# New cost figures for the list scheduler of a mixer block: attention and gated MLP in one kernel

## The chip, the cores and the metric

The kernel runs on one core of a Trainium2 chip. The core has five engines with instruction queues of their own: TensorE (PE, matrix products), VectorE (DVE), ScalarE (ACT), GpSimd (POOL) and SyncE (SP, here only an issuer of DMAs). They meet through semaphores. The metric is the time of one execution on the device in microseconds (us), smaller being better; of several executions the median is given.

## The reference

Two branches share one layer-normalized input and are added to it:

```python
xn = _layernorm(x)                       # x: (1, 2048, 512) bf16
# A: 32 heads of 16; each position attends to 8 earlier ones, 2 apart
q, k, v = split(xn @ wqkv)               # wqkv: 512 x 1536
logits[h, s, w] = sum_d q[h, s, d] * k[h, s - 2*w, d] * 0.25   # w = 0..7, masked before 0
o[h, s] = sum_w softmax(logits)[h, s, w] * v[h, s - 2*w]
A = o @ wo                               # 512 x 512
# B: gelu, a gate that mixes positions, projection
z = gelu(xn @ w_in)                      # 512 x 1792, halves z1 and z2 of 896
g = w_sp @ _layernorm(z2) + b_sp         # w_sp: 2048 x 2048, over positions
B = (z1 * g) @ w_out                     # 896 x 512
out = x + A + B
```

## The kernel before

The 2048 positions are 16 blocks b of 128, or 4 groups j (also called tc) of 512. The program is written as a list of tasks, each with an engine, the keys that it reads and writes, an estimate of its time (`est`) and a name. `Plan.add` turns the keys into dependences. `Plan.schedule` (from line 95) then fixes the order of the tasks on every engine; nothing is reordered at run time. Each engine runs its tasks strictly in that order and waits on semaphores where a dependence is not met, so a task that waits holds up everything behind it on its engine. A DMA is a task of the engine that issues it.

The scheduler keeps a clock for each engine. Again and again it takes, over all engines, the task that can start first by these clocks; of those that could start within `slack` of one another it prefers the class with the lower number (`prio`; the class FILL comes after the default), and then the order in which the tasks were written. A task may carry a `margin`, which is added to the time at which its inputs are ready. `plan.orders` fixes a few orders at the very start by hand. The estimates therefore don't change what an instruction costs on the chip, only who stands before whom.

The work and its names, in the order in which it comes (lines are those of the kernel before):

- **Front.** `ldx` (L533) loads a block of x; `bnst`, `bnag` (L598, L601, DVE), `rstd` (L603, a power on POOL) and `norm` (L605, DVE) normalize it. For blocks 0 to 3 PE transposes (`xTr`, L620), for 4 to 15 the DMA does: `xTd`, L609, issued by SP.
- **Products of xn.** On PE, in this order: `z2_b` (L785) with gelu on ACT (`z2g`, L790, with an accumulated sum; `z2s`, L812, a sum of squares); `Q`, `K` (L665), evicted by ACT (`QKe`, L673); `V` (L647), evicted by ACT (`Ve`, L651) and written to a scratch in memory by POOL's queue (`Vw`, L654); later `z1` (L802) with gelu (L807). `halo` (L679) copies 16 columns on POOL. The layer norm of z2 is `zm`, `zq`, `ze`, `zv` (L818 to L828, DVE), `zr` (L831, a power on POOL) and `zn` (L834, DVE).
- **Attention scores on DVE**, for each group j: four `prod` (L689) and three `padd` (L694), all 128x4096; then a transpose of 1 MB by DMA, `pT` (L706, SP); then `dd0`, `dd1` (L714, L717), the softmax (`sm`, `ssub`, `sexp` on ACT, `sz`, `srec`, `sattn`: L729 to L766) and a trip through memory, `aw` and `al` (L768, L772, POOL's queue).
- **The gate.** `g{fc}_{tc}` (L908) is one group of 16 matmuls over all positions, 7 groups for each tc, 28 in all. Each needs a PSUM bank that ACT has seeded with the bias (`gs`, L902), and w_sp transposed by DMA: `wT` (L841, SP, 2 MB for each tc, in two slots, so that `wT2` waits until group 6 of tc 0 is done, and `wT3` for group 6 of tc 1). `u{fc}_{tc}` (L915, DVE) multiplies the result into z1 and frees the bank; from tc 1 on the groups share four banks.
- **Attention output**, for each j and par in 0, 1: `ldVe` (L925, ACT's queue, 1152 KB) loads V with its shifts; `pv` (two, L933), `pva2048` and `pva1024` (L937) and `pvc` (L941) on DVE form o; `OTd{j}_{par}` (L946, SP, 256 KB) transposes it for two output blocks.
- **Output blocks.** `out{b}` is 4 matmuls with wo (L974) and 7 with w_out (L978), onto a bank that ACT seeds with x (`ldxr`, L962, and `os`, L969); `fin` (L987) evicts and `st` (L990) stores. Blocks 0 and 2 of a group j need `OTd{j}_0`, blocks 1 and 3 `OTd{j}_1`; all need the seven `u` of group j.

SP's queue in the later part reads, in both kernels: ... `pT2`, `ldwout`, four `ldwo`, `wT2`, `pT3`, `OTd0_0`, `wT3`, `OTd0_1`, `OTd1_0`, `OTd1_1`, `OTd2_0`, `OTd2_1`, `OTd3_0`, `OTd3_1`, last store.

Of the kernel before, what the change touches and what calls it, by code (L numbers as in the profile page):

```python
# [6 lines left out]
ENGS = ("pe", "act", "dve", "pool", "sp")  # L7
# [7 lines left out]
class Plan:  # L15
# [79 lines left out]
    def schedule(self, lookahead=64, slack=120.0, dma_bw=300.0, xbar_bw=190.0,  # L95
                 dma_lat=1700.0, issue_ns=None, inv_tol=None, sw_bias=1300.0, verbose=False):
        inv_tol = inv_tol or {"dve": 2400.0}
        issue_ns = issue_ns or {"sp": 650.0, "act": 650.0, "pool": 660.0}
        pending = {e: {} for e in ENGS}
        for t in self.tasks:  # L100
            pending[t.eng].setdefault(t.prio[0], []).append(t)
        for e in ENGS:
            for c in pending[e]:
                pending[e][c].sort(key=lambda t: t.prio)
        byname = {t.name: t for t in self.tasks}
        before = {}
        for names in self.orders:
            for a, b in zip(names, names[1:]):
                assert byname[a].eng == byname[b].eng
                before.setdefault(byname[b], []).append(byname[a])  # L110
        eng_free = {e: 0.0 for e in ENGS}
        dma_free = {e: 0.0 for e in ENGS}
        dma_glob = [0.0]
        order = {e: [] for e in ENGS}
        remaining = len(self.tasks)

        def lat(d, t):
            if d.dma is not None:
                return 150.0
            if d.eng == t.eng:  # L120
                return 35.0
            return 210.0 if d.eng == "pe" else 80.0

        cur_tbl = [None]

        def dur(t):
            if t.dma is not None:
                return issue_ns.get(t.eng, 650.0)
            if t.tbl is not None and t.tbl != cur_tbl[0]:
                return t.est + 1300.0  # L130
            return t.est

        while remaining:
            best = None
            for e in ENGS:
                pl = []
                for c in pending[e]:
                    pl.extend(pending[e][c][:lookahead])
                if not pl:
                    continue  # L140
                cands = []
                for t in pl:
                    ok = all(p.start is not None for p in before.get(t, ()))
                    ready = 0.0
                    for d in t.deps:
                        if d.end is None:
                            ok = False
                            break
                        r = d.end + lat(d, t)
                        if r > ready:  # L150
                            ready = r
                    if ok:
                        st_ = max(eng_free[e], ready + t.margin)
                        if t.tbl is not None and t.tbl != cur_tbl[0] and cur_tbl[0] is not None:
                            st_ += sw_bias
                        cands.append((st_, t))
                if not cands:
                    continue
                pick = None
                pool_c = list(cands)  # L160
                while pool_c:
                    mn = min(c[0] for c in pool_c)
                    near = [c for c in pool_c if c[0] <= mn + slack]
                    P = min(near, key=lambda c: (c[1].prio, c[0]))
                    pend = P[0] + dur(P[1])
                    viol = False
                    for c in cands:
                        if c[1].prio[0] < P[1].prio[0] and pend > c[0] + inv_tol.get(e, 300.0):
                            viol = True
                            break  # L170
                    if not viol:
                        pick = P
                        break
                    pool_c.remove(P)
                if pick is None:
                    pick = min(cands, key=lambda c: (c[1].prio[0], c[0], c[1].prio))
                if best is None or (pick[0], pick[1].prio) < (best[0], best[1].prio):
                    best = pick
            if best is None:
                raise RuntimeError("scheduler stuck (dependency cycle?)")  # L180
            st, t = best
            e = t.eng
            if t.tbl is not None and t.tbl != cur_tbl[0] and cur_tbl[0] is not None:
                st -= sw_bias
            t.start = st
            if t.dma is not None:
                iss = issue_ns.get(e, 650.0)
                t.eng_end = st + iss
                bw = xbar_bw if t.dma.get("xbar") else dma_bw
                xs = max(st + 0.5 * iss, dma_glob[0])  # L190
                xe = xs + t.dma["nbytes"] / bw
                dma_glob[0] = xe
                t.end = max(xe, st + iss) + t.dma.get("lat", dma_lat)
            else:
                t.eng_end = st + dur(t)
                t.end = t.eng_end
                if t.tbl is not None:
                    cur_tbl[0] = t.tbl
            eng_free[e] = t.eng_end
            pending[e][t.prio[0]].remove(t)  # L200
            order[e].append(t)
            remaining -= 1
        self.order = order
        self.makespan = max(t.end for t in self.tasks)
        if verbose:
            self.report()
        return order
# [107 lines left out]
def build_kernel(nc, A_x, A_wqkv, A_wo, B_x, B_w_in, B_w_sp, B_b_sp, B_w_out, out, report=False, sched_kw=None,  # L315
# [12 lines left out]
    FILL = cfg["fill"]  # L328
# [66 lines left out]
    with ExitStack() as es:  # L395
# [92 lines left out]
            return max(25.0, n / 2.4 + 2.6)  # L488

        def c_act(n, psum=True, accum=False):  # L490
            return 165.0 + n * (0.84 if psum else 0.84) + (110.0 if accum else 0.0)

        def c_dve(n, mode=1.0):
            return 130.0 + n / (0.96 * mode)
# [3 lines left out]
        def dma(eng, fn, nbytes, chan, reads=(), writes=(), name="", xbar=False, prio=None, lat=1700.0):  # L498
# [10 lines left out]
          name="steps0")  # L509
# [147 lines left out]
        def qk_pair(j, c):  # L657
            k = next_pair()
            for which in range(2):
                col0 = which * 512 + c  # L660

                def mm(t, col0=col0, which=which):
                    last = None
                    for dc in range(4):
                        last = t.matmul(bank(k + which), AC(off["wqk"] + 1024 * dc + col0, [[4, 128]]),  # L665
                                        AC(off["xnT"] + dc * S + 512 * j, [[1, 512]]), start=(dc == 0),
                                        stop=(dc == 3))
                    return last
                T("pe", mm, reads=[(("wq", "wk")[which], c)] + [("xnT", b) for b in range(4 * j, 4 * j + 4)],
                  writes=[("ps", k + which)], est=4 * c_mm(512), name="%s%d_%d" % ("QK"[which], j, c))  # L670
            qo = q_off(c, j)
            ko = k_off(c, j)
            T("act", lambda a: a.activation(AC(qo, [[ko - qo, 2], [1, 512]]),  # L673
                                            ps[:, 512 * k: 512 * k + 1024].rearrange("p (t n) -> p t n", t=2),
                                            ACTF.Copy, scale=0.5),
              reads=[("ps", k), ("ps", k + 1)], writes=[("QT", c, j), ("KT", c, j)], est=c_act(1024),
              name="QKe%d_%d" % (j, c))
            if j < NJ - 1:
                T("pool", lambda g: g.tensor_copy(AC(k_off(c, j + 1) - KP, [[1, KP]]), AC(ko + 512 - KP, [[1, KP]])),  # L679
                  reads=[("KT", c, j)], writes=[("KTpad", c, j + 1)], est=150, name="halo%d_%d" % (j, c))  # L680

        def prod_reduce(j):
            pa, pb, pc, pl = [(j + i) % NPB for i in range(4)]
# [132 lines left out]
        def z2_wave(j):  # L816
# [12 lines left out]
                                               ALU.subtract),  # L829
              reads=[("msq", j)], writes=[("vpe2", j)], est=160, name="zv%d" % j)  # L830
            T("pool", lambda g: g.tensor_tensor(Fv("rstd2", 4, 4 * j), Fv("vpe2", 4, 4 * j), mhalf, ALU.pow),  # L831
              reads=[("vpe2", j), "mhalf"], writes=[("rstd2", j)], est=900, name="zr%d" % j)
            for b in bl:
                T("dve", (lambda b: lambda v: v.tensor_scalar(A("z2", FH, FH * b), A("z2", FH, FH * b),  # L834
                                                              Fv("m2", 1, b), Fv("rstd2", 1, b), ALU.subtract,
# [84 lines left out]
        def pv_pair(j, par):  # L920
# [3 lines left out]
                          ap=[[4 * 512, 128], [1024, 9], [1, 512]])  # L924
            dma("act", lambda e: e.dma_start(AC(off["Ve"] + 4608 * par, [[512, 9], [1, 512]]), src),  # L925
                128 * 4608 * 2, ("Ve", par), reads=[("vscr", i) for i in range(4 * j - 1, 4 * j + 4)],
                writes=[("Ve", par)], name="ldVe%d_%d" % (j, par), prio=FILL, lat=3400.0)
            nm = "%d_%d" % (j, par)
            for i in range(2):
                iv = AC(off["Ve"] + 4608 * par + (7 + i) * 512, [[-512, 8], [32, 16], [1, 32]])  # L930
# [5 lines left out]
            for n in (2048, 1024):  # L936
# [9 lines left out]
            dma("sp", lambda e: e.dma_start_transpose(AC(off["OT"] + 512 * ob, [[128, 8], [1, 128]]),  # L946
                                                      A("On", 1024, 1024 * so)),
                128 * 1024 * 2, ("OTd", so), reads=[("On", so)], writes=[("OT", ob), ("OT", ob + 1)], name="OTd" + nm,
                xbar=True, lat=3600.0)

        def ot_pos(b):
            return 4 * (b // 4) + 2 * (b % 2) + (b % 4) // 2
# [3 lines left out]
        def out_block(tb, parts=(512,)):  # L956
# [7 lines left out]
            for p_, n in enumerate(parts):  # L964
# [7 lines left out]
                def mm(t, c0=c0, po=po, n=n):  # L972
# [7 lines left out]
                    return last  # L980
                T("pe", mm, reads=[("z1T", fc, tcb) for fc in range(FC)] + ["w_out", ("OT", ot_pos(tb))] + [("wo", c) for c in range(4)],
                  writes=[("ps", k)], est=(FC + 4) * c_mm(n), name="out%d_%d" % (tb, p_),
                  margin=2500.0)
                last_part = p_ > 0
                T("dve" if last_part else "act",
                  (lambda c0, po, n: lambda v: v.tensor_copy(A("yout", n, 512 * sx + c0), po))(c0, po, n) if last_part else
# [82 lines left out]
```

## Time and profile before

| | us |
|---|---|
| median of 3 runs (lowest, highest) | 237.55 (237.34, 238.16) |
| the profiled execution, its own time | 236.66 |
| span of its trace | 234.9 |
| PE busy, share of the span | 231.0, 98% |
| DVE busy | 202.8, 86% |
| ACT busy | 117.5, 50% |
| POOL busy | 50.1, 21% |
| granted TensorE clock | 1.0 |

The page gives busy time by engine, the chain of work that ended last, groups of instructions by line, and the DMA issues with their time to landing. "Idle before, releaser" is what an engine waited for. A time like 145.9 is counted from the start of the span. SPq and ACTq are the queues of SP and ACT as issuers of DMAs: the length of such a row is how long the engine was held by the issue, and the landing comes later.

### The profile page before, as it was taken

To read this page: it belongs to the slowest core of one execution; us is meant where nothing else is said; L and a number is where in the kernel's file an instruction comes from. 1 tells how busy PE (TensorE), PEld (TensorE's weight loads), DVE (VectorE), ACT (ScalarE), POOL (GpSimd) and SP (SyncE) were. 2 spreads that over 40 slices of the span, in tenths; PEclk is the share of its full clock that TensorE was granted. 3 is DMA by queue.
4 is the path that set the end of the run, shared out by engine and by line. 5 is a ranking of instruction groups with operands and counts; after the bars stand their busy time and mean duration, and the time that the engine had idled before them with its cause. 6 is when DMAs were issued, how large, how long until landed. Compare 5 with 4: busy or idle time off the path is not lost.

```text
span 234.9 us, 2932 instructions
## 1 busy us (share of the span) xinstructions
PE 231.0 (98%) x1094; PEld 109.8 (47%) x1094; DVE 202.8 (86%) x230; ACT 117.5 (50%) x227; POOL 50.1 (21%) x67
## 2 busy tenths in 40 slices
PE   7999999999999999999999999999999999999995
PEld 2454455454554444444444444444444444444443
DVE  4789889998989989998999992999999999999600
ACT  2798478998989978962011232324124161201441
POOL 4446944680780050001301000010000000000000
PEclk9999999999999999999999999999999999999999
DMA  7998997390209999796439999999855789702322
GB/s 225 276 360 174 233 225 191 99 171 0 91 3 178 220 231 265 105 253 233 132 87 222 192 312 235 242 181 323 216 156 142 197 268 203 197 3 45 88 69 67
DMA packets 87021, 41.75 MB, mean 178 GB/s; under 512 B 66000, under 2 KB 85856, under 8 KB 87008
## 3 DMA queue, kind: packets, MB, share of 16 engines
q1 hardware_dynamic: 70928, 23.24, 46.5%
q10 hardware_dynamic: 14640, 14.13, 20.8%
q0 software_dynamic: 1440, 4.21, 6.6%
q8 instruction: 8, 0.13, 0.3%
q14 instruction: 5, 0.04, 0.1%
HBM read 20.05 MB, written 5.26 MB: 108 GB/s over the span
## 4 chain that ended last, share of the span: by engine, by line
PE 95%; DMA 2%; DVE 1%; SPq 1%; POOL 0%; issue 0%
PE ps L908 41%; PE ps L665 12%; PE ps L978 10%; PE ps L802 10%; PE ps L785 9%; PE ps L974 6%; PE ps L647 6%; DMA arena<-in_A_x_dram 2%; POOL fpool L603 0%; DVE arena L605 0%; SPq L543 0%; SPq L533 0%; DVE fpool L598 0%; PE ps L620 0%; DVE fpool L601 0%
## 5 line engine op out<-in xcount | busy, mean ns | idle before, releaser
L908 PE MATMUL ps<-arena 128*128 128x512 bf16 x448 | 97.3, 379 | 0.0
L908 PEld LDWEIGHTS ps<-arena 128*128 128x128 bf16 x448 | 43.8, 98 | 52.8
L902 ACT ACTIVATE ps<-arena 128x512 f32<-128x512 bf16 x28 | 16.5, 599 | 57.4 <-DVE arena L915 57.3
L933 DVE TENSOR_TENSOR arena<-arena 128x4096 bf16<-128x4096 bf16 x16 | 36.2, 2286 | 0.4
L689 DVE TENSOR_TENSOR arena<-arena 128x4096 bf16<-128x4096 bf16 x16 | 36.1, 2284 | 0.3 <-ACT arena L673 0.2
L665 PE MATMUL ps<-arena 128*128 128x512 bf16 x128 | 28.3, 379 | 0.0
L937 DVE TENSOR_TENSOR arena<-arena 128x4096 bf16<-128x4096 bf16 (+1 forms) x16 | 28.0, 1753 | 0.2
L694 DVE TENSOR_TENSOR arena<-arena 128x4096 bf16<-128x4096 bf16 x12 | 27.4, 2287 | 0.2
L978 PE MATMUL ps<-arena 128*128 128x512 bf16 (+2 forms) x119 | 27.0, 366 | 0.0
L785 PE MATMUL ps<-arena 128*128 128x448 bf16 x128 | 25.5, 353 | 0.1
L802 PE MATMUL ps<-arena 128*128 128x512 bf16 x112 | 24.3, 379 | 0.0
L665 PEld LDWEIGHTS ps<-arena 128*128 128x128 bf16 x128 | 14.5, 113 | 13.1
L987 ACT ACTIVATE arena<-ps 128x512 bf16<-128x512 f32 (+1 forms) x16 | 9.4, 586 | 21.5 <-PE ps L978 18.6
L673 ACT ACTIVATE arena<-ps 128x1024 bf16<-128x1024 f32 x16 | 16.4, 1022 | 5.7 <-PE ps L665 5.0
L915 DVE TENSOR_TENSOR arena<-ps,arena 128x512 bf16<-128x512 f32 x28 | 19.0, 680 | 0.0
L790 ACT ACTIVATE arena<-ps 128x448 bf16<-128x448 f32 x32 | 17.3, 543 | 2.4
L978 PEld LDWEIGHTS ps<-arena 128*128 128x128 bf16 x119 | 13.1, 113 | 11.4
L785 PEld LDWEIGHTS ps<-arena 128*128 128x128 bf16 x128 | 12.2, 98 | 11.8 <-ACT arena L626 0.6
L807 ACT ACTIVATE arena<-ps 128x512 bf16<-128x512 f32 x28 | 15.9, 595 | 3.2 <-PE ps L802 2.7
L802 PEld LDWEIGHTS ps<-arena 128*128 128x128 bf16 x112 | 11.0, 98 | 13.1
L974 PE MATMUL ps<-arena 128*128 128x512 bf16 (+2 forms) x68 | 16.6, 366 | 0.1
L679 POOL COPY arena<-arena 128x16 bf16<-128x16 bf16 x12 | 14.3, 1197 | 9.9 <-DVE arena L689 7.7
(61 smaller groups left out, 189.2 us busy)
## 6 DMA issues: line engine op xcount, KB each, us to landing
arena<-vscr ACTq DMA_DIRECT2D x8, 1152.0 KB, 7.1
arena<-in_A_x_dram ACTq DMA_DIRECT2D x17, 128.0 KB, 6.1
vscr<-arena POOLq DMA_DIRECT2D x16, 128.0 KB, 2.4
arena<-in_A_x_dram SPq DMA_DIRECT2D x15, 128.0 KB, 4.5
out_dram<-arena ACTq DMA_DIRECT2D x15, 128.0 KB, 3.2
arena<-in_A_wqkv_dram SPq DMA_DIRECT2D x3, 512.0 KB, 5.2
ascr<-arena POOLq DMA_DIRECT2D x4, 256.0 KB, 4.5
arena<-ascr POOLq DMA_DIRECT2D x4, 256.0 KB, 3.7
```

The lines of the kernel that those rows point to most:

```text
L665: last = t.matmul(bank(k + which), AC(off["wqk"] + 1024 * dc + col0, [[4, 128]]), AC(off["xnT"] + dc * S + 512 * j, [[1, 512]]), start=(dc ...
L689: T("dve", lambda v: v.tensor_tensor(pbv, qb, kb, ALU.mult), reads=[("QT", c, j), ("KT", c, j), ("KTpad", c, j)], writes=[("pb", s_)], est ...
L694: T("dve", lambda v: v.tensor_tensor(A("pb", 4096, 4096 * a), A("pb", 4096, 4096 * a), A("pb", 4096, 4096 * b), ALU.add), reads=[("pb", b) ...
L785: last = t.matmul(ps[:, 512 * k: 512 * k + HF], AC(off["xnT"] + dc * S + 128 * b, [[1, 128]]), AC(off["w_in"] + 1792 * dc + c0, [[1, HF]]) ...
L790: T("act", (lambda k, hf: lambda a: a.activation(A("z2", HF, FH * b + HF * hf), ps[:, 512 * k: 512 * k + HF], ACTF.Gelu_apprx_tanh, accum_ ...
L802: lastm = t.matmul(bank(k), AC(off["w_in"] + 1792 * dc + 128 * fc, [[1, 128]]), AC(off["xnT"] + dc * S + 512 * j, [[1, 512]]), start=(dc = ...
L908: last = t.matmul(bank(k), AC(off["z2"] + FH * sh + 128 * fc, [[1, 128]]), AC(off["wT"] + WSL * r_ + sh * 512, [[1, 512]]), start=False, s ...
L915: T("dve", lambda v: v.tensor_tensor(uv, bank(k), uv, ALU.mult), reads=[("ps", k)], writes=[("z1T", fc, tc)], est=c_dve(512) + 20, name="u ...
L933: T("dve", (lambda iv, tv, av: lambda v: v.tensor_tensor(tv, iv, av, ALU.mult))(iv, tv, av), reads=[("attn", j), ("Ve", par)], writes=[("V ...
L937: T("dve", (lambda n: lambda v: v.tensor_tensor(AC(off["Vs"], [[4096, 2], [1, n]]), AC(off["Vs"], [[4096, 2], [1, n]]), AC(off["Vs"] + n, ...
L974: t.matmul(po, AC(off["OT"] + 512 * ot_pos(tb) + 128 * cc, [[1, 128]]), AC(off["wo"] + 512 * cc + c0, [[1, n]]), start=False, stop=False, ...
L978: last = t.matmul(po, AC(off["z1T"] + fc * S + t0, [[ts, 128]]), AC(off["w_out"] + 512 * fc + c0, [[1, n]]), start=False, stop=(fc == FC - ...
```

## The change

Only figures of the scheduler change; no instruction is added, removed or changed in shape. The diff, whole in its code:

```diff
-        issue_ns = issue_ns or {"sp": 650.0, "act": 650.0, "pool": 660.0}
+        issue_ns = issue_ns or {"sp": 470.0, "act": 420.0, "pool": 600.0}
...
-        eng_free = {e: 0.0 for e in ENGS}
+        eng_free = {e: 730.0 for e in ENGS}
...
             if t.dma is not None:
+                if t.dma.get("xbar"):
+                    return max(1250.0, 400.0 + 0.0046 * t.dma["nbytes"])
                 return issue_ns.get(t.eng, 650.0)
...
-                iss = issue_ns.get(e, 650.0)
+                iss = dur(t)
                 t.eng_end = st + iss
-                bw = xbar_bw if t.dma.get("xbar") else dma_bw
-                xs = max(st + 0.5 * iss, dma_glob[0])
-                xe = xs + t.dma["nbytes"] / bw
-                dma_glob[0] = xe
-                t.end = max(xe, st + iss) + t.dma.get("lat", dma_lat)
+                if t.dma.get("xbar"):
+                    dma_glob[0] = max(st, dma_glob[0]) + t.dma["nbytes"] / 450.0
+                    t.end = max(dma_glob[0], st + iss) + 2000.0
+                else:
+                    xs = max(st + 200.0, dma_glob[0])
+                    xe = xs + t.dma["nbytes"] / 340.0
+                    dma_glob[0] = xe
+                    t.end = max(xe, st + iss) + t.dma.get("lat", dma_lat)
...
-            return 165.0 + n * (0.84 if psum else 0.84) + (110.0 if accum else 0.0)
+            return 165.0 + n * (0.84 if psum else 0.84) + (200.0 if accum else 0.0)
...
-                  reads=[("KT", c, j)], writes=[("KTpad", c, j + 1)], est=150, name="halo%d_%d" % (j, c))
+                  reads=[("KT", c, j)], writes=[("KTpad", c, j + 1)], est=1200, name="halo%d_%d" % (j, c))
...
-              reads=[("vpe2", j), "mhalf"], writes=[("rstd2", j)], est=900, name="zr%d" % j)
+              reads=[("vpe2", j), "mhalf"], writes=[("rstd2", j)], est=2500, name="zr%d" % j)
...
-                writes=[("Ve", par)], name="ldVe%d_%d" % (j, par), prio=FILL, lat=3400.0)
+                writes=[("Ve", par)], name="ldVe%d_%d" % (j, par), prio=FILL, lat=2600.0)
...
                 128 * 1024 * 2, ("OTd", so), reads=[("On", so)], writes=[("OT", ob), ("OT", ob + 1)], name="OTd" + nm,
-                xbar=True, lat=3600.0)
+                xbar=True)
...
-                  margin=2500.0)
+                  margin=1500.0)
```

What moves on each engine, by name:

- **PE**: everything up to `g6_1` keeps its place. Before, the order behind it is `g0_2 g1_2 g2_2 out0 out2 g3_2 g4_2 g5_2 g6_2 out1 out3 g0_3 out4 out6 out5 out7 g1_3` and so on. After, it is `out0 out2 g0_2 g1_2 g2_2 g3_2 out1 out3 g4_2 g5_2 g6_2 out4 out6 out5 out7 g0_3 g1_3` and so on. From `g1_3` on the two are the same.
- **DVE**: in the front several `norm`, `bnst` and `bnag` come ahead of `prod0_0`; in the three later waits for `zr1` to `zr3` a `prod`, `padd` or `dd` is put between `zv` and `zn`. In the gate stage the order shifts by one or two places: `padd3_1` stands ahead of `u6_0`; `u1_2` and `u2_2` stand behind `pvc0_1`; `u5_2` and `u6_2` behind `pvc1_1`.
- **ACT**: `QKe` come ahead of `z2s`; `ldVe0_1` moves from the gate stage to just behind `ldVe0_0`; in the gate stage `os0_0` stands ahead of `gs5_1`, `ldVe1_0` behind `os3_0`, and `ldxr4` to `ldxr7` ahead of `gs0_2`.
- **POOL**: some `rstd` and `halo` change places, `al0` comes ahead of `aw1`.
- **SP**: `ldx9` ahead of `ldw_in1`, `xTd5` ahead of `ldx12`, `ldx14` and `ldbbc` behind `xTd11`, `xTd15` ahead of `xTd14`. From `pT0` on the order is the same.

## The prediction

> **What bounds the kernel now.** First the busy times of the page, by engine:
>
> ```profile
> PE 231.0 (98%) x1094; PEld 109.8 (47%) x1094; DVE 202.8 (86%) x230; ACT 117.5 (50%) x227; POOL 50.1 (21%) x67
> ```
>
> PE is busy for all but 3.9 us of a span of 234.9. Next the chain of work that ended last (start, length, what):
>
> ```profile
> 10.34 0.40 PE ps L620 x4
> 10.73 3.03 PE ps L785 x16
> ...
> 97.53 58.71 PE ps L908 x272
> 156.24 0.86 PE ps L974 x4
> 157.10 1.51 PE ps L978 x7
> ...
> 187.75 0.06 issue
> 187.81 1.02 PE ps L974 x4
> 188.84 1.51 PE ps L978 x7
> ```
>
> From 10.34, when the first transpose of normalized x runs, to 232.48 the chain is PE and nothing else, and it is broken once, for 0.06 us ahead of `out5`. One group `g` takes 58.71 / 272 x 16 = 3.45 us, one output block 0.86 + 1.51 = 2.37. The matmuls are the same after the change. So their 222 us stay, what lies in front stays (the orders of SP, DVE, ACT and PE are unchanged up to PE's start), and the last store stays behind `out15`. The change can win only the gap at `out5`; it can lose wherever PE, in its new order, comes to a task whose inputs are not there. The question is which inputs are late.
>
> Third, SP's queue in time order, and VectorE around its one long wait in the gate stage:
>
> ```profile
> 121.73 11.73 SPq L841 DMA_TRANSPOSE arena<-in_B_w_sp_dram  x1
> 133.51 9.78 SPq L706 DMA_TRANSPOSE arena<-arena  x1
> 143.34 2.12 SPq L946 DMA_TRANSPOSE arena<-arena  x1
> 145.91 9.90 SPq L841 DMA_TRANSPOSE arena<-in_B_w_sp_dram  x1
> ```
>
> ```profile
> 139.62 2.28 DVE L933 TENSOR_TENSOR arena<-arena 128x4096 bf16<-128x4096 bf16 x1
> 146.50 1.23 DVE L714 TENSOR_TENSOR arena<-arena 128x2048 bf16<-128x2048 bf16 x1 [4.60 <-DMA arena<-arena]
> ```
>
> The 2 MB `wT2` (L841) may start only when `g6_0` is done, at 97.53 + 7 x 3.45 = 121.7. Issuing it holds SP for 11.73 us, `pT3` (L706) behind it for 9.78, and `OTd0_0` (L946), whose input DVE had ready at 139.06 (`pvc0_0`, 138.37 + 0.69), is issued at 143.34. The trace gives its landing 3.9 us later, 147.28. DVE waits until 146.50 for `pT3` to land. In the old order `out0` reads this transpose at 156.24, 9 us later.
>
> **Part by part.**
>
> *Front and products of xn (up to 97.53).* DVE loses three waits of 0.9 us for `zr1` to `zr3` (2.8 us at L834, released by POOL) and some of the waits for loads, about 1 us by stepping the new order through the old durations; it reaches `padd2_2` some 2 to 4 us earlier. PE gets nothing from that: it never waited for DVE there. Could PE now wait? The last transposes of xn landed at 40.6, and `V12` reads them at 56.95; `xTd14`, now last, is issued about 5 us later than the old last one at most, so 10 us are left. `ldVe0_0` and `ldVe0_1` stand ahead of `QKe1_2` on ACT and wait for `Vw3` (landed at 30.62; `QKe1_2` ran at 32.79): two issues of 0.38 us, below the 3.45 us that two of the eight banks cover. `zn15`, done at 88.4, comes at about 90, due at 97.53. I cost all this at nothing. If one cover failed it would be by parts of a us; with the range below I allow 0 to +0.5.
>
> *Start of tc 1.* `padd3_1` now stands ahead of `u6_0`. `u5_0` waits for `g5_0` (118.25); then 0.6 + 0.65 + 0.95 + 0.6 for the softmax tail and 2.2 for `padd3_1` put `u6_0` at 123.3, done at 124.0, and `gs1_1`, which needs that bank, at 124.6. `g1_1` starts at 97.53 + 8 x 3.45 = 125.16. That leaves 0.5 us: no hold, but the cover is thin; 1 us more on DVE would cost 0.5.
>
> *`out0` and `out2` moved ahead of `g0_2`.* PE reaches `out0` after 14 groups, at 97.53 + 14 x 3.4535 = 145.88. `OTd0_0` stands in the same place of SP's queue, behind the same `wT2`, whose start PE sets at 121.7, and the same `pT3`. VectorE's earlier start doesn't help: SP, not `padd3_2` or `pvc0_0`, is late. Landing again at 147.28, it holds PE. What a hold costs beyond the landing the trace shows at `out5`: the transpose landed at 187.68, the first matmul began at 187.81 (0.13 later), and four matmuls took 1.02 instead of 0.86, since the pipeline was empty. So the hold is 147.28 + 0.13 - 145.88 + 0.16 = **1.69 us**, and nothing behind hides it, because PE runs without gaps to the end.
> The scheduler's new figures say why it dares: a transpose's issue is 400 + 0.0046 x bytes, so 5.2 us for `pT3` and 10.0 for `wT2`; the trace has 9.78 and 11.73 there, 6.3 us more in sum. The figure fits `pT0`, `pT1` (4.88, 4.68), which ran while ACT loaded nothing.
>
> *`out1`, three groups earlier.* Due at 164.44, and at 166.13 with the first hold. `OTd0_1` waits for `pvc0_1`. DVE starts from the same 146.50 and was never idle from there to 182; the new order takes `u1_2` and `u2_2` out of the way: from start to start, one saves 0.48 (2.20 + 0.60 with a `u` between `pva2048` and `pva1024` against 2.32 without), the other 0.42 (0.87 + 0.54 with it behind `srec`, against 0.99). `pvc0_1` ends at 162.27 - 0.90 = 161.37; with the 4.2 us that this transpose took, it lands at 165.6. Not held, by 0.5 us.
>
> *`out5`, one group earlier.* Due at 184.30, with the hold 185.99. `pvc1_1` ends about 0.87 earlier than 182.03 (again two `u` fewer before it), and `OTd1_1`, issued at 181.2, lands 3.0 to 5.6 us later (the fastest and this one in the trace), 184.2 to 186.8. I take no hold: the small loads and stores that ran beside it (`ldxr9`, `ldxr11`, `st1`, `st3`) now come before. Then the old gap, 0.22 with its empty pipeline, is gone. At the other end it is 1.1 us.
>
> *Rest.* The four gate banks of tc 3 are freed over 5 us ahead (`u0_3` ends at about 198, `g4_3` starts at 206); `OTd3_1` landed at 224.44 and `out13` starts at 227.69. Nothing.
>
> *The unknown: how fast `pT3` goes.* It was issued at 133.51 and landed 13.0 us later; `pT0` took 6.8. Beside it ran `ldVe1_0` (1152 KB, issued at 133.83) and the tails of `ldxr0` to `ldxr3`. In the new order these four loads are issued some 2.5 us earlier (`padd3_2` ends at 126.2, not 128.80), `ldVe1_0` behind them and `os3` at 134 to 138, and `ldxr4` to `ldxr7` follow at once, 0.52 MB more. If `pT3` has the engines to itself for a while it may land 2 to 4 us earlier; if the 0.52 MB go first, at the 309 GB/s of the window from 133.5 to 143.3, it lands 1.7 later. I take no change, which is the nearest row (same neighbour, same size), and keep both ends.
> [...]
>
> **Sum.** +1.69 - 0.22 = +1.47. The profiled execution took 236.66, 0.89 below the median of 237.55, so it goes to 238.13, the median to 239.0.
>
> **Rivals.**
> (a) *Not slower.* `pT3` lands at 145.5 or earlier, because `ldVe1_0` starts after it: `OTd0_0` then lands by 146, the hold is 0.4 or none, and only the gap at `out5` goes: -0.2 to +0.7, 237.35 to 238.25. For it: `pT0`'s 6.8 us. Against: `wT2` still moved until 137.4, and `ldVe1_0` needs only `pv0_0_1`, which is earlier too. It decides from 1 us on at `pT3`.
> (b) *Two holds.* `pT3` and `OTd0_0` are slowed by the loads that now follow `ldVe1_0`, by 1.7, or `out5` is held too, by 1.1: 1.47 + 1.1 = +2.6 to 1.47 + 1.7 = +3.2, and with the half us of the front up to +3.7: 240.1 to 241.3. For it: `OTd1_1` is the one transpose that was late before.
> (c) *The change does not do what it says*: figures closer to the trace should give an order with fewer waits, and DVE's waits do shrink; but no wait that shrinks is PE's, and a gain of over 0.7 us (236.8 and below) would need PE to start earlier or to have less work. I see nothing for it but the scatter of the median.
>
> **How the numbers follow.** 0.3% of 237.55 is 0.71 us, about what a measurement of this kernel can tell from no change. Forecast (+0.7 to +2.6): 0.50. Rival (a): 0.20. Rival (b): 0.26. Rival (c): 0.04. Slower is the forecast and (b), 0.76; same is (a), 0.20; faster (c), 0.04. The range takes in (a) and (b) to their ends: 237.3 to 241.3.
>
> **What would show it.** In the profile after: a gap of PE at 145.9 ahead of `out0` (L974 in the old lines), ended by the DMA, and the chain going through SP's queue there. `OTd0_0`'s landing at about 147.3; DVE again idle to 146.5 for `pT3`. No gap at `out1`; at `out5` none or below 1 us. PE's start at 10.3 and everything up to 145.9 without gaps. I am wrong if `pT3`'s issue takes clearly less than 9.8 us, or if PE has gaps before 125, where I found none.

## The result and the profile after

The changed kernel took **240.88 us** (median of 10 runs, 239.19 to 241.56) against 237.57 for the kernel before (10 runs, 236.4 to 238.3): ratio **1.0134** (95% interval 1.0101 to 1.0167). It is slower, in the range given, with a little over twice the loss that was forecast (+3.3 us of medians instead of +1.47). Ratios, here and below, leave out slow runs (those over 1.5% above the fastest of their kernel), so they need not be the ratio of the medians beside them.

The profiled execution after took 241.56, span 239.7, against 236.66 and 234.9. Lines of the kernel after are those of before plus 5 from the transpose figures on (`out` L979 and L983, `g` L913, `OTd` L951, `pT` L711, `wT` L846, `ldVe` L930). First the busy times of the page after:

```profile
PE 231.6 (97%) x1075; PEld 110.0 (46%) x1094; DVE 203.2 (85%) x230; ACT 117.4 (49%) x227; POOL 52.6 (22%) x67
```

The work is the same (the lower matmul count is missing records), only the span is longer: the 4.8 us are PE's idle and slow time. The chain that ended last, around `out0` (start, length, what):

```profile
137.94 1.99 DVE arena L938
139.92 9.15 DMA arena<-arena
149.11 1.87 PE ps L979 x4
150.99 2.36 PE ps L983 x7
...
155.72 9.06 PE ps L913 x42
```

Before, the chain was PE from the front to the end. Now it leaves PE at 132.46, for 7.4 us of DVE and then a DMA that took 9.15 us from issue to landing: `OTd0_0`. (The DVE rows are how the view links the chain. The input of `OTd0_0`, `pvc0_0`, was done at 137.84; what ended last ahead of its issue at 139.92 was the issue of `pT3` on SP's queue, at 133.16 + 6.71 = 139.87, as the rows below show.) PE's own timeline there (start, length; idle before and its releaser in brackets):

```profile
137.68 8.58 PE L913 MATMUL ps<-arena 128*128 128x512 bf16 x38
149.11 1.87 PE L979 MATMUL ps<-arena 128*128 128x512 bf16 x4 [2.85 <-DMA arena<-arena]
150.78 2.57 PE L983 MATMUL ps<-arena 128*128 128x512 bf16 x7
```

Two losses stand here. PE stood still for 2.85 us ahead of `out0`. Then the four matmuls took 1.87 instead of the 0.86 of the chain before. The granted clock tells why, in the view by stretches (stretch, its length, then busy time of PE, PEld, DVE, ACT, POOL, the granted clock, DMA share, GB/s):

```profile
145.87:149.11 3.24, 0.39 (x2) 0.00 (x1) 3.21 (x4) 0.13 (x1) 0.00 (x0) 1.00 1.13 289
149.11:152.35 3.24, 3.24 (x8) 1.18 (x9) 3.14 (x5) 1.53 (x2) 0.00 (x0) 0.51 1.26 281
152.35:155.72 3.37, 3.32 (x15) 1.64 (x15) 3.23 (x7) 1.72 (x3) 0.00 (x0) 0.97 1.28 291
```

Over the 3.24 us after the stand-still PE got a clock of 0.51. Cut finer, the same view has 0.50 from 149.17 to 152.58, which is 3.41 us, and 1.00 on both sides. SP's queue, as it was shown of the kernel before:

```profile
122.12 11.00 SPq L846 DMA_TRANSPOSE arena<-in_B_w_sp_dram  x1
133.16 6.71 SPq L711 DMA_TRANSPOSE arena<-arena  x1
139.92 1.50 SPq L951 DMA_TRANSPOSE arena<-arena  x1
146.29 8.09 SPq L846 DMA_TRANSPOSE arena<-in_B_w_sp_dram  x1
```

`pT3` was issued in 6.71 us instead of 9.78, so `OTd0_0` went out 3.4 us earlier, and yet landed 1.8 us later (139.92 + 9.15 = 149.07; before 143.34 + 3.9 = 147.28). `pT3` itself, though issued faster, landed hardly earlier: DVE, which waits for it, went on at 145.86 instead of 146.50.

```profile
145.86 1.23 DVE L719 TENSOR_TENSOR arena<-arena 128x2048 bf16<-128x2048 bf16 x1 [5.03 <-DMA arena<-arena]
```

What the DMA engines moved from 139.92 to 149.07, by queue (packets, MB, share of the 16 engines; q10 carries what ACT issues, q1 what SP issues):

```profile
q10 hardware_dynamic: 1744, 1.70, 66.8%
q1 hardware_dynamic: 3332, 0.84, 49.8%
```

The 1.70 MB are the 1664 KB of `ldVe1_0` and of `ldxr4` to `ldxr7`, all of which thus moved while `OTd0_0` was on its way.

**The sum.** Front: PE started at 10.72 instead of 10.34 (+0.38; one load, with nothing changed ahead of it, landed 0.38 later; `lds_late`, below, has the same front and reaches the first `g` at 97.22, so this is scatter and not the change). `out0` was due at 97.91 + 14 x 3.4535 = 146.26: hold +2.85. `out0` and `out2` took 6.61 us (149.11 to 155.72) instead of 4.75: +1.86, of which 0.16 is the empty pipeline (1.02 instead of 0.86 for four matmuls, as read at `out5` before) and 1.70 the half clock. The old gap at `out5` is gone: -0.22. Together +4.87, for a span that grew by 4.8. Of the ten executions two kept a clock of 1.0 throughout; they had a span of 237.4 and took 239.19 and 239.2. The other eight show a mean clock of 0.993 and took 240.98 in the mean, 1.79 more: about the size of the third term.

### The profile page after: what moved, and what is told of

The parts are those of the page before. It is cut to its first block, busy times and chain, and to the rows that moved or that the text cites. A ratio compares the mean times of both kernels' runs of the same rounds, so it can differ in the third digit from the quotient of the medians.

```text
span 239.7 us, 2915 instructions
## 1 busy us (share of the span) xinstructions
PE 231.6 (97%) x1075; PEld 110.0 (46%) x1094; DVE 203.2 (85%) x230; ACT 117.4 (49%) x227; POOL 52.6 (22%) x67
## 4 chain that ended last, share of the span: by engine, by line
PE 87%; DMA 6%; DVE 4%; SPq 1%; issue 1%; POOL 0%; DVEq 0%
PE ps L913 34%; PE ps L670 12%; PE ps L983 10%; PE ps L807 10%; PE ps L790 9%; PE ps L979 6%; PE ps L652 6%; DMA arena<-arena 4%; DMA arena<-in_A_x_dram 2%; DVE arena L942 1%; DVE arena L938 1%; DVE arena L920 1%; POOL fpool L608 0%; DVE arena L610 0%; SPq L548 0%
## 5 line engine op out<-in xcount | busy, mean ns | idle before, releaser
L913 PE MATMUL ps<-arena 128*128 128x512 bf16 x440 | 96.9, 379 | 0.4
L913 PEld LDWEIGHTS ps<-arena 128*128 128x128 bf16 x448 | 43.8, 98 | 52.8
L983 PE MATMUL ps<-arena 128*128 128x512 bf16 (+2 forms) x117 | 27.8, 375 | 0.2
L979 PE MATMUL ps<-arena 128*128 128x512 bf16 (+2 forms) x66 | 17.2, 381 | 2.9 <-DMA arena<-arena 2.9
L983 PEld LDWEIGHTS ps<-arena 128*128 128x128 bf16 x119 | 13.3, 115 | 12.4 <-issue 1.6
L684 POOL COPY arena<-arena 128x16 bf16<-128x16 bf16 x12 | 14.8, 1246 | 8.5 <-DVE arena L694 8.4
```

Source lines behind the costliest of these rows:

```text
L913: last = t.matmul(bank(k), AC(off["z2"] + FH * sh + 128 * fc, [[1, 128]]), AC(off["wT"] + WSL * r_ + sh * 512, [[1, 512]]), start=False, s ...
L979: t.matmul(po, AC(off["OT"] + 512 * ot_pos(tb) + 128 * cc, [[1, 128]]), AC(off["wo"] + 512 * cc + c0, [[1, n]]), start=False, stop=False, ...
L983: last = t.matmul(po, AC(off["z1T"] + fc * S + t0, [[ts, 128]]), AC(off["w_out"] + 512 * fc + c0, [[1, n]]), start=False, stop=(fc == FC - ...
```

## The experiments

The theory: the new place of `out0` makes the whole loss, `OTd0_0` lands late because `ldVe1_0` (1152 KB on ACT's queue) now goes out just ahead of it, and the half clock comes from the stand-still. ACT's queue after shows how `ldVe1_0` got there:

```profile
136.05 0.60 ACT L974 ACTIVATE ps<-arena 128x512 f32<-128x512 bf16 x1 [7.92 <-DMA arena<-in_A_x_dram]
...
137.45 0.38 ACTq L930 DMA_DIRECT2D arena<-vscr  x1
```

`os0_0` waits 7.92 us for `ldxr0`, which was issued at 126.64 beside `wT2` and landed 9.4 us later; `ldVe1_0` is queued behind it and goes out at 137.45 instead of 133.83. The rivals: the four loads `ldxr4` to `ldxr7` behind it do it; or the changed orders of DVE, ACT, SP or the front cost something too.

Except for the two with changed figures (`no_xbar`, `xbar_only`), each kernel is the one after with its order on every engine written out in `plan.orders` as the scheduler had made it (with its `lookahead` lifted for that), and then edited as shown. Ratios are to the kernel before on the same chip.

### Only PE's order put back: `pe_old`

```diff
-  PE:  g6_1 out0 out2 g0_2 g1_2 g2_2 g3_2 out1 out3 g4_2 g5_2 g6_2 out4 ... out7 g0_3
+  PE:  g6_1 g0_2 g1_2 g2_2 out0 out2 g3_2 g4_2 g5_2 g6_2 out1 out3 g0_3 out4 ... out7
```

> The changed kernel with all its orders, only TensorE's order is that of the kernel before (out0, out2 behind g2_2, out1, out3 behind g6_2, g0_3 ahead of out4). Theory 1 (the whole cost is the hold of TensorE ahead of out0, with the half clock that follows it): no hold at out0, granted clock 1.00 throughout, span about 235, time within 0.3% of the kernel before. Rival (the new orders of VectorE, ScalarE and the loads cost something by themselves, or the front is 0.4 us later because of the change): the time stays 0.4 us or more above the kernel before, with gaps elsewhere.

Measured: 236.49 (12 runs, 236.28 to 237.4), ratio 0.9981 (0.9963 to 1.0); span 234.5, clock 1.0. PE has no gap left in the gate stage. `OTd0_0` was still slow, issued at 139.81 and landing 9.8 us later, at 149.6, but `out0` came at 155.91:

```profile
142.75 13.33 PE L913 MATMUL ps<-arena 128*128 128x512 bf16 x61
155.91 1.03 PE L979 MATMUL ps<-arena 128*128 128x512 bf16 x4
```

All other moves of the change, in the front, on DVE, ACT, POOL and SP, thus cost nothing, and gain at the most 0.4%. The loss is PE's order.

### `out0` one group later: `out0_g1`

```diff
-  PE:  g6_1 out0 out2 g0_2 g1_2 ...
+  PE:  g6_1 g0_2 out0 out2 g1_2 ...
```

> The changed kernel with out0 and out2 one group later on TensorE, behind g0_2 instead of ahead of it; everything else as changed. Theory 1 with the measured landing: out0 is then due 3.45 us later, near 149.5, and OTd0_0 lands near 149.1 (148.6 to 149.1 in the runs so far): hold 0 to 0.3 us, clock 1.00, time within 0.3% of the kernel before. So one group of matmuls between is enough cover. Rival (the place matters further on, in the freeing of banks or at out1): over 0.7 us above the kernel before.

Measured: 237.69 (9 runs, 236.71 to 238.45), ratio 1.0035 (1.0014 to 1.0055), clock 1.0 in all. `OTd0_0` landed 9.8 us after its issue at 140.14, so at 149.9, and PE stood still for 0.59 us at `out0`, where 0 to 0.3 had been expected, and for 0.4 more at `out5`, without a half clock. One group (3.45 us) covers most of the lateness of `OTd0_0`, not quite all.

### The four small loads later: `ldxr_late`

```diff
-  ACT: os3_0 ldVe1_0 gs6_1 ldxr4 ldxr6 ldxr5 ldxr7 gs0_2 gs1_2 gs2_2 sexp3
+  ACT: os3_0 ldVe1_0 gs6_1 gs0_2 gs1_2 gs2_2 ldxr4 ldxr6 ldxr5 ldxr7 sexp3
```

> The changed kernel, only ldxr4 to ldxr7 (0.52 MB of residual loads) are put back behind gs2_2 on ScalarE's queue, so that they are issued after 148. Theory 2a (these four loads are what slows the transpose OTd0_0): at about 280 KB per us they are worth 1.9 us, OTd0_0 lands near 147.2 instead of 149.1, the hold at out0 is about 1 us, the clock stays at 1.00, and the time is 1.0 to 1.5 us above the kernel before. Theory 2b (ldVe1_0 with its 1152 KB is what slows it): OTd0_0 still lands at 148 or later, hold over 2 us, time about as the changed kernel.

Measured: 240.23 (6 runs, 238.59 to 243.0), ratio 1.0112 (1.0065 to 1.0159). `OTd0_0`, issued at 140.45, landed 8.1 us later. PE's timeline:

```profile
148.63 1.02 PE L979 MATMUL ps<-arena 128*128 128x512 bf16 x4 [2.46 <-issue]
149.49 2.98 PE L983 MATMUL ps<-arena 128*128 128x512 bf16 x7
```

The hold is 2.46 instead of 2.85, and in this execution the half clock follows it (2.98 for seven matmuls, where `out2` takes 1.67). Of the six, three kept a clock of 1.0 and took 238.59 to 239.46, against 239.19 and 239.2 of the kernel after with a full clock. The four loads are a small part of the cause, not the cause.

### All the loads later: `lds_late`

```diff
-  ACT: os3_0 ldVe1_0 gs6_1 ldxr4 ldxr6 ldxr5 ldxr7 gs0_2 gs1_2 gs2_2 sexp3
+  ACT: os3_0 gs6_1 gs0_2 gs1_2 gs2_2 ldVe1_0 ldxr4 ldxr6 ldxr5 ldxr7 sexp3
```

> The changed kernel, with ldVe1_0 and ldxr4 to ldxr7 all put behind gs2_2 on ScalarE's queue (issued after 148, so after OTd0_0 is through). Theory 2 (loads on ScalarE's queue, issued before OTd0_0, set its landing): OTd0_0, issued near 140, lands 3 to 4.5 us later, by 144.5, before TensorE reaches out0 at 146; no hold, clock 1.00, time within 0.3% of the kernel before and at best 0.2 us below it. Rival (the place behind wT2 and pT3 in SyncE's queue sets it, as the prediction had it): landing at 147 or later, a hold of 1.5 us or more, time at 239 or above.

Measured: `OTd0_0`, with no load beside it, landed 3.1 us after its issue at 139.77, and `out0` was not held, as the theory wants. But the time is 261.02 (6 runs, 254.6 to 262.41; too scattered for a ratio). `ldVe1_0` went out at 145.34, 0.3 us ahead of `wT3` on SP's queue:

```profile
139.77 1.31 SPq L951 DMA_TRANSPOSE arena<-arena  x1
145.60 35.17 SPq L846 DMA_TRANSPOSE arena<-in_B_w_sp_dram  x1
180.81 4.17 SPq L951 DMA_TRANSPOSE arena<-arena  x2
```

The issue of `wT3` held SP for 35.17 us instead of 8.09. `OTd0_1` is queued behind it, and PE waited for it at `out1`:

```profile
185.70 1.89 PE L979 MATMUL ps<-arena 128*128 128x512 bf16 x4 [21.58 <-DMA arena<-arena]
```

The step wanted was shown, and the expected time missed by 24 us, since the expectation priced nothing behind it. After, the loads went out around `OTd0_0` (landing 9.15 us behind its issue, 3.1 here); here they went out around `wT3` (issue 35.17 us, 8.09 after).

### `ldVe1_0` between the two: `ve_mid`

```diff
-  ACT: os3_0 ldVe1_0 gs6_1 ldxr4 ldxr6 ldxr5 ldxr7 gs0_2 gs1_2 gs2_2 sexp3
+  ACT: os3_0 gs6_1 gs0_2 gs1_2 ldVe1_0 gs2_2 ldxr4 ldxr6 ldxr5 ldxr7 sexp3
```

> The changed kernel; ldVe1_0 moves behind gs1_2 on ScalarE's queue (issue near 141, just after OTd0_0 is issued near 140 and well ahead of wT3 at 146), ldxr4 to ldxr7 behind gs2_2. Theory 2 (ldVe1_0, in flight when OTd0_0 is issued, delays it): with nothing in flight at 140 OTd0_0 lands 3 to 4 us after its issue, near 143.5, TensorE is not held at out0, the clock stays at 1.00, wT3's issue takes 8 to 10 us, and the time is 0 to 0.5 us below the kernel before. Rival (the two transfers share the engines whichever is issued first): OTd0_0 lands at 146.5 or later and holds TensorE by 0.5 us or more; or wT3 is stretched as in the run with all loads late, and the loss returns at out1.

Measured: 253.24 (6 runs, 239.13 to 254.35; too scattered for a ratio). Both things named as the rival came. `ldVe1_0` went out at 140.47, 0.3 us behind `OTd0_0`, which then took 6.6 us to land; `out0` was held for 0.98, with a full clock behind it. `wT3` was issued at 145.96 together with `ldxr4` to `ldxr7` and took 19.27, and `out1` was held for 12.59. The run at 239.13 (clock 1.0), 13.7 us below the profiled one at 252.86, can't have had that hold: this stretch is not the same in every execution.

### `ldVe1_0` earlier: `ve_early`

```diff
-  ACT: ldxr1 ldxr3 os0_0 gs5_1 os2_0 os1_0 os3_0 ldVe1_0 gs6_1
+  ACT: ldxr1 ldxr3 ldVe1_0 os0_0 gs5_1 os2_0 os1_0 os3_0 gs6_1
```

> The changed kernel; ldVe1_0 moves ahead of os0_0, so that it is issued when VectorE has read the buffer, near 132, as in the kernel before, and not near 137.4. Theory 2: it then runs beside pT3 instead of beside OTd0_0; pT3's issue takes 8 to 10 us again, OTd0_0 is issued near 143 and lands near 147.3 as in the kernel before, the hold is 1 to 1.7 us, the clock stays at 1.00, and the time is 1.0 to 1.7 us above the kernel before. This is the case that the prediction priced at +1.5. Rival (ldxr4 to ldxr7, still ahead, decide): OTd0_0 lands at 148.5 or later, hold over 2.4 us, clock halved, time as the changed kernel.

Measured: 242.67 (4 runs, 241.77 to 243.24), ratio 1.0242 (1.0213 to 1.0271): slower still, where it had been expected to be better. `ldVe1_0` went out at 131.96 and met `pT3`:

```profile
134.52 11.55 SPq L711 DMA_TRANSPOSE arena<-arena  x1
146.12 1.31 SPq L951 DMA_TRANSPOSE arena<-arena  x1
```

`pT3` took 11.55 us to issue, `OTd0_0` went out only at 146.12 and, with ACT's loads landed by then (the last at 145.57), landed 3.8 us later. `out0` was held for 3.98. So none of the places tried for this load (issued at 131.96, 137.45, 140.47 and 145.34) mends the kernel with `out0` where it now stands: only the last feeds `out0` in time, and then `out1` waits.

### `ldVe1_0` made small: `ve_small`

It loads one of the nine rows of `ldVe1_0` (128 KB); eight ninths of the V of group 1, par 0 are left out, so its output is not the block's.

```diff
-                ap=[[4 * 512, 128], [1024, 9], [1, 512]])
+                ap=[[4 * 512, 128], [1024, 1 if (j, par) == (1, 0) else 9], [1, 512]])
```

> The changed kernel with ldVe1_0 cut to one of its nine rows (128 KB instead of 1152), in its place; the attention output of group 1, par 0 is then computed from old data in the other rows, so a part of the computation is left out. ldxr4 to ldxr7 stay ahead. Theory 2b (ldVe1_0 is what delays OTd0_0): OTd0_0 lands 3 to 5.5 us after its issue near 140, so by 145.5; no hold at out0, clock 1.00, time within 0.3% of the kernel before. Rival (ldxr4 to ldxr7 or SyncE's own pace are enough): it lands at 147 or later, a hold of over 1 us remains, time at least 1 us above the kernel before.

Measured: 237.18 (10 runs, 236.55 to 237.47), ratio 1.0013 (0.9995 to 1.0032), clock 1.0 in all. `OTd0_0`, issued at 139.85 in nearly the same instant as after, landed 6.4 us later, at 146.27 (expected by 145.5):

```profile
146.41 1.02 PE L979 MATMUL ps<-arena 128*128 128x512 bf16 x4 [0.80 <-DMA arena<-arena]
147.27 1.67 PE L983 MATMUL ps<-arena 128*128 128x512 bf16 x7
```

With 1024 KB gone, most of the loss is gone. Set side by side, the landing of `OTd0_0` grows with what ACT's queue had under way. Counted are the KB of `ldVe1_0` and `ldxr4` to `ldxr7` issued from 136.6 until 1 us behind `OTd0_0`; each row is one execution, the profiled one, of each kernel named (`fill12`, `fill4` and `xbar_only` follow below):

| kernel | KB | `OTd0_0`, issue to landing |
|---|---|---|
| `lds_late`; `xbar_only` | 0 | 3.1; 3.7 us |
| `ve_small` | 640 | 6.4 us |
| `ldxr_late` | 1152, ahead of it | 8.1 us |
| `ve_mid` | 1152, 0.3 us behind it | 6.6 us |
| after; `fill12`; `fill4`; `pe_old`, `out0_g1` | 1664 | 9.15; 9.0; 8.8; 9.8, 9.8 us |

In `xbar_only` `ldVe1_0` went out 1.5 us behind `OTd0_0`. From 0 to 1664 KB (`lds_late` to after) it is 6 us, which is 280 GB/s, and 279 GB/s is what the trace after shows for 139.92 to 149.07. By that rate from the 3.1 us of `lds_late` on, `ve_small` would be at 5.4 and `ldxr_late` at 7.3; they lie 1.0 and 0.8 us above.

### Zero work ahead of `out0`: `fill12` and `fill4`

Twelve, then four matmuls with weights of zero are added on the bank of `out0`, between `g6_1` and `out0`. They wait for nothing that is late, add zero to the result, and only keep PE running.

```diff
+                if tb == 0:
+                    def fillz(t, po=po):
+                        for _ in range(12):        # fill4: range(4)
+                            last = t.matmul(po, A("zz", 128), A("w_out", 512), start=False, stop=False, skip_group_check=True)
+                        return last
```

> The changed kernel with 12 extra matmuls (128x512, zero weights, added onto the bank of out0) between g6_1 and out0, 2.6 us of work inside the hold of 2.85 us; a 128-column tile of zeros is set once by GpSimd. The result is not altered by adding zeros. Theory 3 (TensorE's clock is halved because it stood still for 2.85 us, and that costs 1.9 us more): the granted clock stays at 1.00 behind out0, the 22 matmuls of out0 and out2 go back to 0.216 us each, and the time is about 1.5 to 1.9 us below the changed kernel, 239.0 to 239.4. Rival (the matmuls behind the hold are slow because transfers were still running, or for another reason than the standing still): they stay slow and the time stays at 240.9, or rises.

Measured: 239.31 (6 runs, 239.06 to 240.35), ratio 1.0098 (1.0065 to 1.013); span 237.5 and a clock of 0.999 or 1.0 in every run. `fillz` is L990, `out0` L980 and L984:

```profile
145.67 2.75 PE L990 MATMUL ps<-arena 128*128 128x512 bf16 x12
148.53 1.02 PE L980 MATMUL ps<-arena 128*128 128x512 bf16 x4
149.39 1.67 PE L984 MATMUL ps<-arena 128*128 128x512 bf16 x7
```

`OTd0_0` landed as late as ever (139.45 + 9.0), and `out0` began at 148.53, but with no stand-still there is no half clock: four matmuls 1.02, seven 1.67.

> The changed kernel with only 4 of the extra matmuls with zero weights ahead of out0, 0.86 us of work, so that TensorE stands still for some 1.6 to 2.0 us instead of 2.5 to 2.9. Theory 3: the clock is halved only behind a stand-still that reaches into the order of 2.5 us (2.46 and 2.85 did it, 0.98 and 0.06 did not): it stays at 1.00 in all or most runs, and the time is that of the run with 12 extra matmuls, 239.3 with the kernel before at 236.75 (+2.5). Rival (any stand-still over a us can do it): 0.98 to 0.993 of mean clock in most runs and +3.3 or more.

Measured: 239.36 (4 runs, 239.12 to 241.27), ratio 1.0126 (1.009 to 1.0162). The profiled run stood still for 1.67 us and kept a full clock; three runs of four show a clock of 1.0 and take 239.12 to 239.59, the fourth shows 0.993 and takes 241.27. In `fill12`, without the stand-still, no execution of six shows a clock below 0.999; after, with 2.85 us of it in the profiled one, eight of ten show 0.993. So the half clock comes from the stand-still, and about 1.8 us hang on whether it comes. By the medians of the kernels this is not resolved (the intervals of after, `fill4` and `fill12` overlap); the executions of one kernel, with and without it, show it.

### The figures of the transposes alone: `no_xbar`, `xbar_only`

`no_xbar` is the kernel after with the old figures for transposes (issue, rate, landing, and the 3600 of `OTd`), all the other new ones kept. `xbar_only` is the reverse: the kernel before with the new figures of the transposes and nothing else.

```diff
 no_xbar, against after:
-                if t.dma.get("xbar"):
-                    return max(1250.0, 400.0 + 0.0046 * t.dma["nbytes"])
...
-                    t.end = max(dma_glob[0], st + iss) + 2000.0
+                    t.end = max(dma_glob[0], st + iss) + t.dma.get("lat", dma_lat)
```

> The changed kernel with its new figures for DMA transposes taken back (issue, end and the landing of OTd as in the kernel before); all other new figures stay, margin 1500 and the longer GpSimd times too. The scheduler then puts out0 behind g1_2. Theory 1 (the place of out0 is all): out0 is reached near 152.9, OTd0_0 is there, no hold, time within 0.3% of the kernel before. Rival (the other figures cost too): a gap at another place and 0.7 us or more above the kernel before.

Measured: 236.58 (10 runs, 236.19 to 237.71), ratio 1.0003 (0.9979 to 1.0026). The scheduler puts `out0` behind `g1_2`, it starts at 152.33, and nothing is held.

> The kernel before with the new figures for DMA transposes alone; every other figure is the old one, margin 2500 too. The scheduler puts out0 behind g6_1, as in the changed kernel, and ldVe1_0 behind gs6_1 on ScalarE's queue. Theory 1 and 2: the whole loss comes with this one part: OTd0_0 lands 8 to 9 us after its issue, TensorE is held by 2 to 3 us at out0, with or without the half clock behind it, time 2 to 4 us above the kernel before. Rival (the loss needs the other figures as well): less than 1 us above the kernel before.

Measured: 244.22 (4 runs, 243.33 to 245.45), ratio 1.0323 (1.029 to 1.0355): 7.5 us above the kernel before, where 2 to 4 had been expected, and at another place. Here too `out0` stands ahead of `g0_2`. It happens to be fed in time (`OTd0_0` issued at 139.20, landed 3.7 us later, with `ldVe1_0` out only at 140.68), but that load still ran when `wT3` was issued; `wT3` took 12.16, and `OTd0_1` went out at 157.94 and landed 13.3 us later:

```profile
171.31 1.89 PE L979 MATMUL ps<-arena 128*128 128x512 bf16 x4 [7.05 <-DMA arena<-arena]
```

So it is the transposes' figures that draw the output blocks forward, and it is chance, the place of one load, which of them is then late.

## Why the prediction was right, and where it was not

**Right: that PE's new order can only lose.** In the gate stage PE has no other new gap than the one at `out0`; the start of tc 1, `out1` and `out5` are not held, as each step said, and `OTd0_1` landed at 164.2, ahead of the 165.6 forecast. `pe_old` shows it from the other side: with PE's old order nothing is lost, and DVE's shorter waits bring next to nothing. (Under *Rest*, the 206 for `g4_3` should be 204.5 by the prediction's own steps, 192.72 + 3 x 3.4535 + 1.47; its bank was free at 198.7 in the trace after, so nothing hangs on it.)

**Right: the place.** `out0` waits for `OTd0_0`, 14 groups after 97.9, and nothing hides the wait. That the figures for transposes bring `out0` there is confirmed by `no_xbar` and `xbar_only`. Which of them does it, the 5.2 us for the issue of `pT3` or another, was not tested; that figure is nearer to the new order (6.71, and 5.48 in `lds_late`) than to the old (9.78). The old gap at `out5` went, as put down.

**Wrong: why, and so when, `OTd0_0` lands late.** The step was "Landing again at 147.28": SP's queue busy with `pT3` until 143.34, and 3.9 us more. Both terms failed, in opposite directions. `pT3` held SP for 6.71 us instead of 9.78, because `ldVe1_0`, issued at 137.45 instead of 133.83, no longer ran beside its whole length (`ve_early`, with the load at 131.96, puts it back there: 11.55). The prediction had named this as a sign that it is wrong: "if `pT3`'s issue takes clearly less than 9.8 us". (Its "I take no change" held for the landing of `pT3`, 12.7 us behind its issue against 13.0, but not for the issue.) So it is not SP's queue that is late: in `lds_late` `OTd0_0` was issued at the same time, 139.77, met no load, landed at 142.9, and `out0` was not held. But after, the load was not gone; under way from 137.45 to 146.9, it now met the end of `pT3` (landed at 145.84), and `OTd0_0`, whose 3.9 us had been read where ACT's queue had just run empty (`ldVe1_0` landed at 143.93 there). `OTd0_0` took 9.15. It lands 6.2 us later than in `lds_late`, 3.2 us behind `pT3`, which stands ahead of it on the same queue. The hold is 2.85 instead of 1.69. The 1.8 us between the two landings are thus what is left of two errors, 3.4 us too late and 5.2 too short, and that `out0` was held at all, and the time in the range, is in part luck. The trace of before had what was needed: by its 309 GB/s the 1152 KB of `ldVe1_0` are 3.8 us, and they had to go somewhere. The prediction put the load's new time rightly at "134 to 138", but priced only `ldxr4` to `ldxr7` against `OTd0_0`, not this load.

**Missing: the half clock.** The term after the hold was the 0.16 of an empty pipeline, read at the gap of 0.06 at `out5`. Behind a gap of 2.85 it was 1.86, the same 0.16 and 1.70 of half clock; by the mean clocks the half clock came in eight executions of ten. A short gap is no row for a long one.

**Rivals.** (b) gave 240.1 to 241.3 and holds the median, in part for the wrong reason: `OTd0_0` was slowed by loads, but chiefly by `ldVe1_0`, not by those that "follow" it (`ldxr_late`: 0.39 us of hold), `pT3` landed no later than before, `out5` was not held, and the half clock makes up the rest. (a) asked for a `pT3` landed at 145.5 or earlier; it landed at 145.84, and `OTd0_0` 3.2 us behind it. (c) fell.

**The extra loads.** The prediction added nothing for `ldxr4` to `ldxr7`, and kept 1.7 as its upper end. `ldxr0` (128 KB), issued at 128.83 beside `wT2`, landed 7.1 us later in the trace before; in the trace after, issued at 126.64, it landed 9.4 us later, 2.9 us behind the end of the issue of `wT2`. In the same trace, from 142 to 146, ACT's queue moved 879 packets, 0.89 MB, beside 576, 0.14 MB, of SP's. What decides between the two queues is not shown. The upper end, 1.69 + 1.7 = 3.4, would have been nearer to the measured 2.85 + 0.16.

**Left open.** Why the issue of `wT3` takes 12.61 us in `no_xbar`, where `ldxr4` to `ldxr7` went out from 0.09 us behind its start on, and 7.62 in `ldxr_late`, where they went out 4.08 us behind it; and why the half clock comes in some executions of a kernel and not in others. The landings and stand-stills are those of one profiled execution of each kernel. No version here is clearly faster than the kernel before; `pe_old`, at 0.9981, has 1.0 for the end of its interval.

## What to carry to other kernels

When a scheduler's new figures move work forward, ask of every transfer that it then needs what else will be in flight at that moment: here a load taken off `pT3` (issue 6.71 us instead of 9.78) landed on `OTd0_0` (9.15 instead of 3.9), and its 1152 KB by the 309 GB/s of the window, 3.8 us, were the price that was missing. Figures that fit the undisturbed rows of a trace (here `pT0` and `pT1`) make an order that has no slack where the rows are disturbed; 9 us of unused slack at `out0` were what made the old order safe. And a stand-still of TensorE like the 2.85 us here is priced with the half clock that may follow it (1.70 us), not with the wait alone.

## What the runs showed of the hardware

- **Transposes on SP's queue beside plain loads on ACT's.** The issue of the 2 MB `wT3` took 7.45 us in `ve_small`, 7.62 in `ldxr_late`, 7.73 in `ve_early`, 8.09 after (ACT's queue moved 0.43 MB in it), 9.90 before (0.37 MB), 12.16 in `xbar_only`, 12.61 in `no_xbar`, 19.27 in `ve_mid` and 35.17 in `lds_late`. In the last four ACT's queue had these loads out around its start: `ldVe1_0` 5.05 us ahead of it and `ldxr4` to `ldxr7` behind that, the last 2.62 us ahead, in `xbar_only`; `ldxr4` to `ldxr7` from 0.09 us behind it on in `no_xbar` and from 0.20 us ahead of it on in `ve_mid`; `ldVe1_0` 0.26 us ahead and `ldxr4` to `ldxr7` from 0.16 us behind in `lds_late`. `ldVe1_1`, which follows on ACT's queue, falls into all four (issued at 149.17 to 151.28). In `lds_late` the engines were not idle: the trace shows 221 and then 157 GB/s (145.6 to 160, 160 to 180). The issue of the 1 MB `pT3` took 5.48 us in `lds_late`, where ACT issued no load in it, 6.71 after (ACT's queue moved 0.51 MB), 9.78 before (1.70 MB), and 11.55 in `ve_early`, with `ldVe1_0` issued 2.56 us ahead of it and `ldxr4` to `ldxr7` in it.
- **The order of the issues.** In `lds_late` `ldVe1_0` went out 0.26 us ahead of `wT3` and landed after 7.6 us; `wT3` landed after 39.1. In `ldxr_late` 512 KB of loads went out 4.08 us behind `wT3`, and its issue ended after 7.62 us.
- **Stand-stills and the clock.** Behind stand-stills of 2.46, 2.85, 3.98, 7.05, 12.6 and 21.6 us PE ran at half rate (`ldxr_late`, after, `ve_early`, `xbar_only`, `ve_mid`, `lds_late`); behind 0.06, 0.4, 0.59, 0.80, 0.98 and 1.67 us it did not (before, `out0_g1` twice, `ve_small`, `ve_mid`, `fill4`). After, the half rate (a granted clock of 0.50) lasted 3.41 us, from 149.17 to 152.58. For the others the mean clock c of the profiled execution gives an estimate, 2 x (1 - c) x span: 3.3 us in `ldxr_late` (0.993, 239.2), 6.8 in `ve_early` (0.986, 241.4), 6.8 in `xbar_only` (0.986, 243.0), 13.6 in `ve_mid` (0.973, 251.1) and 20.6 in `lds_late` (0.960, 258.0). It need not begin where PE resumes: in `ldxr_late` PE resumed at 148.63, and the first four matmuls took 1.02, the next seven, from 149.49, 2.98; in `lds_late` the mean clock was 0.73 from 160 to 180, though PE stood still from 164.1 to 185.70. What sets the length, and what decides whether it comes, is not shown.
